# q loaded in 2 KB pieces and sorted at eviction, with an earlier start of the products, smaller preparation steps and half-row stores, in a fused attention and expert-merge kernel

## Chip, cores, metric

One core of one Trainium2 chip. The metric is the device time of one execution, in microseconds. The six runs of the kernel before lie within 0.3% (1258.14 to 1261.69 us). Each chip job also ran the kernel before on the same chip, several times. A ratio is the mean time of one kernel's fast runs over that of the kernel before in the same rounds, with a 95% interval. So it is not quite the ratio of the medians that are quoted beside it. Line numbers such as L347 differ between kernels, because the text above them differs. L93 is in all of them a helper that issues every tensor-tensor operation, so those are told apart by their tiles. In the views PE is TensorE, PEld its weight loads, DVE VectorE, ACT ScalarE, POOL GpSimd and SP the engine that issues most loads. In this kernel TensorE writes its results to PSUM, to tiles that the code calls banks; an **eviction** is the copy or addition that moves a result from PSUM to SBUF, the on-chip memory, and frees the bank.

## The reference

```python
# lightning attention: B=4, H=8, S=768, D=64, fp32, chunk by chunk
intra = (q_b k_b^T * decay mask) v_b
inter = (q_b * lam^(pos+1)) kv_state
kv_state = lam^block * kv_state + (k_b * lam^(block-1-pos))^T v_b
x = (intra + inter) as (B*S, H*D) = (3072, 512)
# then 4 experts, F = 1024, weighted by normalised domain probabilities
out = sum_e p_e * (relu(x @ w1[e]) @ w2[e])
```

All inputs are fp32 in HBM. q, k and v lie as (batch, head, token, 64), so one row of a head is 256 B, and consecutive tokens of one head are contiguous.

## The kernel before

The kernel takes 128 tokens at a time (a chunk, all 8 heads) and writes the attention's result, transposed, to `xT`. Eight chunks make a group of 1024 tokens. Both expert products use Strassen-like schemes of seven products (M1 to M7). The sums that they need of x, w1 and w2 are made by GpSimd and VectorE as "chores" that a function `pump` issues between matmuls. The results go to HBM and are fetched again just ahead of use. The first group's attention runs alone (the **opening**, about the first 110 us). The other two groups' attention is spread in small steps between the matmuls of the expert products (the **middle**).

The parts that the change touches, with cuts marked by `...`:

```python
def load(n):                                   # 128 tokens of q, k, v
    b, c = divmod(n, NCH)
    for name, src in (("q", q), ("k", k), ("v", v)):
        x = small(f"{name}n")[:].rearrange("p (h d) -> p h d", d=D)
        nc.sync.dma_start(out=x, in_=src[b, :, c*C:(c+1)*C, :].rearrange("h p d -> p h d"))
...
def pump():                                    # the stores of the last chore, then one chore
    for f in stores: f()
    stores.clear()
    if chores: chores.pop(0)()
...
def turn(n, tags):                             # transpose q and k of a chunk
    for x, y in ((qp, qn), (kp, kn)):
        for hp in range(NHP):
            nc.tensor.transpose(out=x[:, hp*C:(hp+1)*C], in_=y[:, 2*hp:2*hp+2]..., identity=ident[:])
    nc.scalar.copy(out=qT[:], in_=qp[:])       # one copy of 128x512
    nc.scalar.copy(out=kT[:], in_=kp[:])
    if n % NCH:
        tt(nc.vector, qs[:], qT[:], q_decay..., ALU.mult)
...
def scores(n, tags):   # TensorE: k^T q per head; VectorE: st = scores * mask
def values(n, tags):   # TensorE: result and new kv; ScalarE: copy to xT; VectorE: kv update
...
for x, part in enumerate(order):               # one product of a unit: 8 places
    ...
    if x in (1, 4, 6):
        pump()
```

Of the kernel before, what the change touches and what calls it, by code (L numbers as in the profile page):

```python
# [20 lines left out]
def kernel(  # L21
# [30 lines left out]
    nc = tc.nc  # L52
# [45 lines left out]
    def load(n):  # L98
        b, c = divmod(n, NCH)
        tiles = []  # L100
        for name, src in (("q", q), ("k", k), ("v", v)):
            x = small(f"{name}n")[:].rearrange("p (h d) -> p h d", d=D)
            nc.sync.dma_start(out=x, in_=src[b, :, c * C:(c + 1) * C, :].rearrange("h p d -> p h d"))  # L103
            tiles.append(x)
        nat[n] = tiles
# [3 lines left out]
    lam_hp = consts.tile([P, NHP], FP32, name="lam_hp")  # L109
    for hd in range(2):  # L110
        nc.scalar.dma_start(
            out=lam_hp[half[hd], :], in_=lam.rearrange("(hp hd) -> hd hp", hd=2)[hd].partition_broadcast(D),
        )
# [56 lines left out]
    def prepare_w1(e):  # L170
# [13 lines left out]
        def ready(m):  # L184
# [5 lines left out]
            lambda: (total("S1", "A21", "A22", ALU.add), ready("M5")),  # L190
            lambda: (total("S3", "A11", "A21", ALU.subtract), ready("M7")),
            lambda: (total("S2", "S1", "A11", ALU.subtract), block("A12", 0, 1), ready("M6")),
            lambda: ready("M2"),
            lambda: (total("S4", "A12", "S2", ALU.subtract), ready("M3")),
# [41 lines left out]
    def prepare_x(g):  # L236

        st = {}

        def total(name, a, b, op):  # L240
            t = stage.tile([P, 2, W], FP32, name="xo", tag="st")
            tt(nc.gpsimd, t[:], a, b, op)
            st[name] = t[:]

        def ready(m, blk):
            inner_x(nc.gpsimd, g, m, blk)

        return [lambda: ready("M1", b11), lambda: ready("M2", b21)], [
            lambda: (total("T1", b12, b11, ALU.subtract), ready("M5", st["T1"])),
            lambda: (total("T2", b22, st["T1"], ALU.subtract), ready("M6", st["T2"])),  # L250
            lambda: (total("T3", b22, b12, ALU.subtract), ready("M7", st["T3"])),
            lambda: ready("M3", b22),
            lambda: (total("T4", b21, st["T2"], ALU.subtract), ready("M4", st["T4"])),
        ]
# [29 lines left out]
    for n in range(4):  # L284
        load(n)
    for name in ("A21", "A22", "A11"):
        raw_w1(0, name)
    probs = consts.tile([P, NTOK // P, E], FP32, name="probs")
    nc.scalar.dma_start(out=probs[:], in_=moe_domain_probs.rearrange("(t p) e -> p t e", p=P))
# [16 lines left out]
    nc.vector.tensor_copy(out=q_decay[:, :, 0], in_=lam_hp[:])  # L306
# [11 lines left out]

    gate = consts.tile([P, NTOK // P, E], FP32, name="gate")
# [16 lines left out]
    def turn(n, tags):  # L336
        qn, kn, _ = nat[n]
        qp = bank(tags[0], "qp")
        kp = bank(tags[1], "kp")
        for x, y in ((qp, qn), (kp, kn)):  # L340
            for hp in range(NHP):
                nc.tensor.transpose(  # L342
                    out=x[:, hp * C:(hp + 1) * C], in_=y[:, 2 * hp:2 * hp + 2].rearrange("p h d -> p (h d)"),
                    identity=ident[:],
                )
        qT, kT, qs = small("qT"), small("kT"), None
        nc.scalar.copy(out=qT[:], in_=qp[:])  # L347
# [26 lines left out]
    def values(n, tags):  # L374
        _, kn, vn = nat.pop(n)
# [198 lines left out]
    def second_product(g, e, m, banks):  # L574

        def part(sj, s):
# [29 lines left out]
            if e == E - 1 and m in ("M5", "M3"):  # L606
                nc.gpsimd.dma_start(out=out[n * P:(n + 1) * P, :], in_=acc.pop(n)[0][:])  # L607
# [16 lines left out]
    def direct_product(e, m, blocks, tags):  # L624
# [6 lines left out]
        def quarter(at):  # L631
# [9 lines left out]
            new[at] = small("m" + at) if m in ("M1", "M2", "M5") else blocks[old][at]  # L641
            if old is None:
# [10 lines left out]
    between, blocks = [], {}  # L653
    for i in range(CPG + 2):
        if i == 3:
            sum_w1(0, "S1", "A21", "A22", ALU.add)
            sum_w1(0, "S3", "A11", "A21", ALU.subtract)
        if i == 4:
# [3 lines left out]
        if i > 4:  # L662
            pump()
        if i == 6:
            between = direct_product(0, "M1", blocks, ("g1", "g3"))
        for f, lag in ((scores, 1), (turn, 0), (values, 2)):
# [3 lines left out]
            if i == 7 and lag == 0:  # L670
                between += direct_product(0, "M2", blocks, ("g1", "g3"))
            if between:
                between.pop(0)()
        if i + 4 < CPG:
            load(i + 4)
        if i == 0:
            raw_w1(0, "A12")
        if i == 6:
            gates()

    def sum_x(name, a, b):
        t = stream.tile([P, 7, 256], FP32, name="xt", tag="xw"[len(x_now) % 2])
        x_now[name] = t[:, 0:4].rearrange("p (c a) t -> p c (a t)", c=2)
        tt(nc.vector, x_now[name], x_now[a], x_now[b], ALU.subtract)

    sum_x("T1", "B12", "B11")
    sum_x("T2", "B22", "T1")
    sum_x("T3", "B22", "B12")
    sum_x("T4", "B21", "T2")
    for f in between:  # L690
        f()
    chores.extend(lambda n=n: raw_w1(1, n) for n in ("A11", "A12", "A21", "A22"))
    chores.append(lambda: sum_w1(1, "S1", "A21", "A22", ALU.add))
    for m in SEQ0[2:]:
# [9 lines left out]
        lambda: sum_w1(1, "S3", "A11", "A21", ALU.subtract), own[1], w2_steps[0],  # L704
        lambda: sum_w1(1, "S4", "A12", "S2", ALU.subtract), own[2], w2_steps[1],
        own[3], w2_steps[2], w2_steps[3], own[4], w2_steps[4], w1_steps[0], own[5], *w1_steps[1:3], own[6], *w1_steps[3:],
# [6 lines left out]
    for at, (g, e) in enumerate(units):  # L713
# [9 lines left out]
        for i in range(7):  # L723
# [11 lines left out]
            for x, part in enumerate(order):  # L735
# [10 lines left out]
                if x in (1, 4, 6):  # L746
                    pump()
    assert not (background or chores or stores or acc)
# [28 lines left out]
```

## Time and profile before

| | before |
|---|---|
| time, median of the first 3 runs | 1260.18 us |
| span of the profiled run | 1257.4 us |
| TensorE busy | 1226.8 us (98%) |
| TensorE waits | 25.7 us, of which 16.1 in the opening |
| tail after the last matmul | 4.9 us |

TensorE bounds the kernel, so what counts is its idle time. A line of waits reads "engine, tile and line, what it waited for: us in total, times, longest us". A line of stretches reads "window, length, busy us of PE, PEld, DVE, ACT and POOL with their instructions, granted clock, DMA share, GB/s". A line of a tile or group gives count and min/median/max of the duration in ns.

```profile
L347 ACT COPY qT<-qp x24: 566/585/592, 5.8 to 674.6; 128x512 f32<-128x512 f32 x24
```

```profile
DVE qs L93 <- ACT qT L347: 13.6, 16, 3.2
```

The first line has a granted clock of 0.83: TensorE idles here for 3.3 us ahead of the first matmul that needs a sum of x. The line of L347 is the single copy that evicts q, 585 ns.

### The profile page before, as it was taken

What the parts mean: (1) busy time and instruction counts of PE and PEld (TensorE: products, weight loads), DVE (VectorE), ACT (ScalarE), POOL (GpSimd) and SP (SyncE); (2) the same over time, 40 slices, a digit from 0 to 9 for tenths busy, and PEclk for the clock granted to TensorE, in tenths of its full rate; (3) what the DMA queues carried; (4) which work ended last, traced back from release to release, by engine and by line L of the source; (5) the groups of instructions that cost most, each with busy time, mean ns of one, the idle gap of its engine ahead of it and who ended that gap; (6) DMA issues with size and microseconds to landing.
All of it is one profiled execution on the core that took longest, in us unless ns stands there. A gap on an engine that the chain in (4) does not pass through costs nothing.

```text
span 1257.4 us, 16224 instructions
## 1 busy us (share of the span) xinstructions
PE 1226.8 (98%) x6376; PEld 1071.3 (85%) x6376; DVE 762.4 (61%) x1267; ACT 217.1 (17%) x361; POOL 301.1 (24%) x294
## 2 busy tenths in 40 slices
PE   6989999999999999999999999999999999999998
PEld 5878888888888888888888888888888888888887
DVE  4656478477467745756764674674764755755742
ACT  2213102111202211220221021120120120220100
POOL 3620236586356683112000700000010000000001
PEclk9999999999999999999999999999999999999999
DMA  9741477999999799667544764454565445454412
GB/s 187 209 151 47 166 251 270 374 317 382 307 341 348 225 328 362 214 222 237 176 176 151 265 232 177 175 202 154 217 224 199 178 174 203 154 217 156 167 59 93
DMA packets 173052, 273.10 MB, mean 217 GB/s; under 512 B 87600, under 2 KB 120496, under 8 KB 172976
## 3 DMA queue, kind: packets, MB, share of 16 engines
q1 hardware_dynamic: 143808, 212.37, 50.6%
q10 hardware_dynamic: 27248, 53.41, 11.3%
q0 software_dynamic: 1920, 6.29, 1.3%
q8 instruction: 50, 0.82, 0.3%
q14 instruction: 26, 0.21, 0.1%
HBM read 212.39 MB, written 59.64 MB: 216 GB/s over the span
## 4 chain that ended last, share of the span: by engine, by line
PE 47%; issue 42%; DMA 5%; POOL 2%; SPq 2%; DVE 1%; ACT 0%; ACTq 0%; POOLq 0%; DVEq 0%
PE q L589 18%; PE pg L537 14%; PE pM L637 7%; PE op L389 2%; PE sp L365 2%; PE kvp L398 2%; SPq L103 1%; PE op L383 1%; DMA xs_in<-x_ops 1%; DMA x_ops<-xo 1%; DMA w2t<-in_moe_w_dram 1%; POOL ops L93 1%; POOL out_dram L607 1%; PE qp L342 1%; DMA kn<-in_k_dram 1%
## 5 line engine op out<-in xcount | busy, mean ns | idle before, releaser
L537 PE MATMUL pg<-xs_in,ws_in 128*128 128x256 f32 x1960 | 470.9, 380 | 6.6 <-DVE m L93 3.4
L537 PEld LDWEIGHTS pg<-xs_in,ws_in 128*128 128x128 f32 x1960 | 369.2, 190 | 60.3 <-DVE m L93 5.6
L589 PE MATMUL q<-w2t,hS 128*128 128x256 f32 x1536 | 361.0, 379 | 0.0
L93 DVE TENSOR_TENSOR m<-pg,m 128x512 f32<-128x512 f32 x410 | 280.1, 688 | 92.9 <-PE pg L537 79.2
L589 PEld LDWEIGHTS q<-w2t,hS 128*128 128x128 f32 x1536 | 291.1, 190 | 39.9
L605 DVE SCALAR_TENSOR_TENSOR acc<-q,gate,acc 128x256 f32<-128x256 f32 x288 | 138.9, 482 | 234.6 <-PE q L589 234.2
L589 PE MATMUL q<-w2t,m 128*128 128x256 f32 x1152 | 270.7, 379 | 0.0
L589 PEld LDWEIGHTS q<-w2t,m 128*128 128x128 f32 x1152 | 218.5, 190 | 29.7
L607 POOL DMA_DIRECT2D out_dram<-acc x24 | 13.2, 550 | 548.6 <-DVE acc L605 548.6
L549 ACT ACTIVATE m<-m 128x512 f32<-128x512 f32 x120 | 75.4, 630 | 361.9 <-DVE m L93 349.7
L93 DVE TENSOR_TENSOR hS<-m,m 128x512 f32<-128x512 f32 x96 | 68.8, 719 | 20.9 <-ACT m L549 20.9
L545 ACT COPY m<-pg 128x512 f32<-128x512 f32 x80 | 46.5, 585 | 174.9 <-PE pg L537 157.1
L93 DVE TENSOR_TENSOR m<-m,m 128x512 f32<-128x512 f32 x96 | 73.8, 773 | 0.0
L93 POOL TENSOR_TENSOR kn<-kn,s_decay 128x256 f32<-128x256 f32 x40 | 30.1, 773 | 114.1 <-PE kp L342 110.9
L491 ACT ACTIVATE m<-m 128x512 f32<-128x512 f32 x48 | 29.9, 629 | 152.3 <-DVE m L93 147.7
L637 PE MATMUL pM<-xt,w1o 128*128 128x256 f32 x192 | 45.6, 391 | 4.8 <-DVE xt L93 3.3
L637 PEld LDWEIGHTS pM<-xt,w1o 128*128 128x128 f32 x192 | 37.2, 196 | 10.7 <-DVE xt L93 3.5
L602 DVE TENSOR_SCALAR acc<-q,gate 128x256 f32<-128x256 f32 x48 | 23.1, 482 | 37.2 <-PE q L589 37.1
L93 DVE TENSOR_TENSOR m<-pM,m 128x512 f32<-128x512 f32 x40 | 27.4, 687 | 24.9 <-PE pM L637 24.8
L93 DVE TENSOR_TENSOR st<-sp,s_decay 128x512 f32<-128x512 f32 x48 | 30.8, 684 | 11.4 <-PE sp L365 11.2
L93 DVE TENSOR_TENSOR hS<-hS,m 128x512 f32<-128x512 f32 x48 | 35.3, 736 | 0.5
L93 POOL TENSOR_TENSOR w2o<-w2b 128x1024 f32<-128x1024 f32 x8 | 18.9, 2364 | 69.4 <-DMA w2b<-in_moe_w_dram 49.9
(65 smaller groups left out, 777.4 us busy)
## 6 DMA issues: line engine op xcount, KB each, us to landing
xs_in<-x_ops SPq DMA_DIRECT2D x70, 896.0 KB, 4.6
ws_in<-w_ops SPq DMA_DIRECT2D x70, 896.0 KB, 6.6
w2t<-w_sums SPq DMA_DIRECT2D x96, 256.0 KB, 6.4
w2t<-in_moe_w_dram SPq DMA_DIRECT2D x72, 256.0 KB, 6.6
w_ops<-ops ACTq DMA_DIRECT2D x28, 512.0 KB, 6.8
x_ops<-ops ACTq DMA_DIRECT2D x21, 512.0 KB, 5.0
w2b<-in_moe_w_dram SPq DMA_DIRECT2D x32, 256.0 KB, 5.6
w_sums<-w2o ACTq DMA_DIRECT2D x16, 512.0 KB, 6.7
```

The lines of the kernel that those rows point to most:

```text
L93: eng.tensor_tensor(out=o, in0=a, in1=b, op=op)
L365: nc.tensor.matmul(out=sp[hd][:, hp * C:(hp + 1) * C], lhsT=hc(kT)[half[hd], hp], rhs=hc(qT)[half[hd], hp], start=True, stop=True,)
L389: nc.tensor.matmul(out=op[half[hd], hp * C:(hp + 1) * C], lhsT=vn[:, 2 * hp + hd], rhs=hc(st[hd])[:, hp], start=(first and hp == 0), stop= ...
L398: nc.tensor.matmul(out=kpv[:, hp], lhsT=kn[:, 2 * hp:2 * hp + 2].rearrange("p h d -> p (h d)"), rhs=vn[:, 2 * hp:2 * hp + 2].rearrange("p ...
L491: nc.scalar.activation(out=o[:], in_=o[:], func=AF.Relu)
L537: nc.tensor.matmul(out=p[:, j * 256:(j + 1) * 256], lhsT=ws[:, W1_AT[i], j * P:(j + 1) * P], rhs=xs[:, X_AT[i]], start=(fresh and j == 0), ...
L545: nc.scalar.copy(out=new[at][:], in_=p[:])
L549: nc.scalar.activation(out=new[at][:], in_=new[at][:], func=AF.Relu)
L589: nc.tensor.matmul(out=p[:, s * DH:(s + 1) * DH], lhsT=h[A_OF[m]][:, c * 256 + s * P:c * 256 + (s + 1) * P], rhs=fed2[g, e, m][uu][:, c], ...
L605: nc.vector.scalar_tensor_tensor(out=o, in0=x, scalar=w, in1=o, op0=ALU.mult, op1=ALU.add)
L607: nc.gpsimd.dma_start(out=out[n * P:(n + 1) * P, :], in_=acc.pop(n)[0][:])
L637: nc.tensor.matmul(out=p[:, s * 256:(s + 1) * 256], lhsT=a[c][:, f:f + P], rhs=b[:, c, j * 256:(j + 1) * 256], start=(s == 0 and c == 0), ...
```

## The change

The intent: start the opening earlier, fill its gaps with matmuls that need no sum of x, keep GpSimd from falling behind, and shorten the tail. The diff, cut to its core:

```diff
-    def load(n):
+    def load(n, names="qkv"):
...
+            if name == "q":      # partition = (head, block of 8 tokens): 128 pieces of 2 KB
+                nc.sync.dma_start(out=x[:], in_=src.rearrange("h (tb ti) d -> h tb (ti d)", ti=TI))
-    lam_hp = consts.tile([P, NHP], FP32, name="lam_hp")       # and its two loads
...
-    for n in range(4):
-        load(n)
-    for name in ("A21", "A22", "A11"):
-        raw_w1(0, name)
-    nc.scalar.dma_start(out=probs[:], ...)                    # now after iteration 5
+    for n, names in ((0, "qk"), (1, "qk"), (0, "v"), (2, "qk"), (1, "v")):
+        load(n, names)
+    raw_w1(0, "A11")
+    load(3, "qk")
...
     def turn(n, tags):
-        nc.scalar.copy(out=qT[:], in_=qp[:])
+        to = qT[:].rearrange("p (hp tb u r) -> p r u hp tb", hp=NHP, tb=TB, r=2)
+        of = qp[:].rearrange("p (u hp hd tb) -> p hd u hp tb", u=TI // 2, hp=NHP, hd=2)
+        for hd in range(2):
+            for r in range(2):
+                nc.scalar.copy(out=to[half[hd], r], in_=of[half[r], hd])   # 4 copies of 64x256
...
-            lambda: (total("S1", "A21", "A22", ALU.add), ready("M5")),
+            lambda: total("S1", "A21", "A22", ALU.add), lambda: ready("M5"),      # and the like
...
-            if e == E - 1 and m in ("M5", "M3"):
-                nc.gpsimd.dma_start(out=out[n * P:(n + 1) * P, :], in_=acc.pop(n)[0][:])
+            if e == E - 1 and m in ("M2", "M4", "M5", "M3"):
+                queue = nc.sync if (g, m) == (NG - 1, "M3") else nc.gpsimd
+                queue.dma_start(out=out[n * P:(n + 1) * P, j * DH:(j + 1) * DH], in_=o)
...
+    between = {4: (m1[0], m1[2]), 5: (m2[0], m2[2]), 6: (m1[1],), 7: (m1[3],), 8: (m2[1],), 9: (..., m2[3])}
...
-                if x in (1, 4, 6):
+                if x % 2 == 0:
                     pump()
```

More of the change, by code (lines that the diff above doesn't have):

```diff
@@ L96 @@
     nat = {}
-    def load(n):
+    TI = 8
+    TB = C // TI
+    def load(n, names="qkv"):
         b, c = divmod(n, NCH)
-        tiles = []
-        for name, src in (("q", q), ("k", k), ("v", v)):
-            x = small(f"{name}n")[:].rearrange("p (h d) -> p h d", d=D)
-            nc.sync.dma_start(out=x, in_=src[b, :, c * C:(c + 1) * C, :].rearrange("h p d -> p h d"))
-            tiles.append(x)
-        nat[n] = tiles
+        for name in names:
+            x = small(f"{name}n")
+            src = {"q": q, "k": k, "v": v}[name][b, :, c * C:(c + 1) * C, :]
+            if name == "q":
+                nc.sync.dma_start(out=x[:], in_=src.rearrange("h (tb ti) d -> h tb (ti d)", ti=TI))
+                nat[n, name] = x
+            else:
+                nat[n, name] = x[:].rearrange("p (h d) -> p h d", d=D)
+                nc.sync.dma_start(out=nat[n, name], in_=src.rearrange("h p d -> p h d"))
     lam_bc = consts.tile([P, H], FP32, name="lam_bc")
     nc.scalar.dma_start(out=lam_bc[:], in_=lam.partition_broadcast(P))
-    lam_hp = consts.tile([P, NHP], FP32, name="lam_hp")
-    for hd in range(2):
-        nc.scalar.dma_start(
-            out=lam_hp[half[hd], :], in_=lam.rearrange("(hp hd) -> hd hp", hd=2)[hd].partition_broadcast(D),
-        )
     w1_ops = dram.tile([E, 7, P, 7, 256], FP32, name="w1_ops")
@@ L189, in prepare_w1 @@
             lambda: ready("M1"),
-            lambda: (total("S1", "A21", "A22", ALU.add), ready("M5")),
-            lambda: (total("S3", "A11", "A21", ALU.subtract), ready("M7")),
-            lambda: (total("S2", "S1", "A11", ALU.subtract), block("A12", 0, 1), ready("M6")),
+            lambda: total("S1", "A21", "A22", ALU.add), lambda: ready("M5"),
+            lambda: total("S3", "A11", "A21", ALU.subtract), lambda: ready("M7"),
+            lambda: (total("S2", "S1", "A11", ALU.subtract), block("A12", 0, 1)), lambda: ready("M6"),
             lambda: ready("M2"),
-            lambda: (total("S4", "A12", "S2", ALU.subtract), ready("M3")),
+            lambda: total("S4", "A12", "S2", ALU.subtract), lambda: ready("M3"),
             lambda: ready("M4"),
@@ L248, in prepare_x @@
         return [lambda: ready("M1", b11), lambda: ready("M2", b21)], [
-            lambda: (total("T1", b12, b11, ALU.subtract), ready("M5", st["T1"])),
-            lambda: (total("T2", b22, st["T1"], ALU.subtract), ready("M6", st["T2"])),
-            lambda: (total("T3", b22, b12, ALU.subtract), ready("M7", st["T3"])),
+            lambda: total("T1", b12, b11, ALU.subtract), lambda: ready("M5", st["T1"]),
+            lambda: total("T2", b22, st["T1"], ALU.subtract), lambda: ready("M6", st["T2"]),
+            lambda: total("T3", b22, b12, ALU.subtract), lambda: ready("M7", st["T3"]),
             lambda: ready("M3", b22),
-            lambda: (total("T4", b21, st["T2"], ALU.subtract), ready("M4", st["T4"])),
+            lambda: total("T4", b21, st["T2"], ALU.subtract), lambda: ready("M4", st["T4"]),
         ]
@@ L282, in sum_w1 @@
         w1_now[e][name] = to
-    for n in range(4):
-        load(n)
-    for name in ("A21", "A22", "A11"):
-        raw_w1(0, name)
-    probs = consts.tile([P, NTOK // P, E], FP32, name="probs")
-    nc.scalar.dma_start(out=probs[:], in_=moe_domain_probs.rearrange("(t p) e -> p t e", p=P))
+    for n, names in ((0, "qk"), (1, "qk"), (0, "v"), (2, "qk"), (1, "v")):
+        load(n, names)
+    raw_w1(0, "A11")
+    load(3, "qk")
+    load(2, "v")
+    raw_w1(0, "A12")
+    load(3, "v")
+    raw_w1(0, "A21")
+    raw_w1(0, "A22")
     s_decay = consts.tile([P, 2, NHP, C], FP32, name="s_decay")
@@ L305 @@
     q_decay = consts.tile([P, NHP, C], FP32, name="q_decay")
-    nc.vector.tensor_copy(out=q_decay[:, :, 0], in_=lam_hp[:])
+    for hd in range(2):
+        nc.vector.tensor_copy(
+            out=q_decay[half[hd], :, 0], in_=lam_bc[half[hd], :].rearrange("p (hp hd) -> p hd hp", hd=2)[:, hd],
+        )
     m = 1
@@ L317 @@
     nc.vector.memset(kv[:], 0.0)
+    probs = consts.tile([P, NTOK // P, E], FP32, name="probs")
     gate = consts.tile([P, NTOK // P, E], FP32, name="gate")
@@ L336, in turn @@
     def turn(n, tags):
-        qn, kn, _ = nat[n]
+        qn, kn = nat.pop((n, "q")), nat[n, "k"]
         qp = bank(tags[0], "qp")
         kp = bank(tags[1], "kp")
-        for x, y in ((qp, qn), (kp, kn)):
-            for hp in range(NHP):
-                nc.tensor.transpose(
-                    out=x[:, hp * C:(hp + 1) * C], in_=y[:, 2 * hp:2 * hp + 2].rearrange("p h d -> p (h d)"),
-                    identity=ident[:],
-                )
-        qT, kT, qs = small("qT"), small("kT"), None
-        nc.scalar.copy(out=qT[:], in_=qp[:])
+        for hp in range(NHP):
+            nc.tensor.transpose(out=qp[:, hp * C:(hp + 1) * C], in_=qn[:, hp * C:(hp + 1) * C], identity=ident[:])
+        for hp in range(NHP):
+            nc.tensor.transpose(
+                out=kp[:, hp * C:(hp + 1) * C], in_=kn[:, 2 * hp:2 * hp + 2].rearrange("p h d -> p (h d)"),
+                identity=ident[:],
+            )
+        qT, kT, qs = small("qT"), small("kT"), None
+        to = qT[:].rearrange("p (hp tb u r) -> p r u hp tb", hp=NHP, tb=TB, r=2)
+        of = qp[:].rearrange("p (u hp hd tb) -> p hd u hp tb", u=TI // 2, hp=NHP, hd=2)
+        for hd in range(2):
+            for r in range(2):
+                nc.scalar.copy(out=to[half[hd], r], in_=of[half[r], hd])
         nc.scalar.copy(out=kT[:], in_=kp[:])
@@ L374, in values @@
     def values(n, tags):
-        _, kn, vn = nat.pop(n)
+        kn, vn = nat.pop((n, "k")), nat.pop((n, "v"))
         qs = turned.pop(n)[2]
@@ L641, in quarter @@
             new[at] = small("m" + at) if m in ("M1", "M2", "M5") else blocks[old][at]
+            if m == "M1":
+                blocks[m] = new
             if old is None:
@@ L652, with x_sums @@
     pairs = (("s0", "s1"), ("q01", "q02"), ("q11", "q12"))
-    between, blocks = [], {}
+    def x_sums():
+        for name, a, b in (("T1", "B12", "B11"), ("T2", "B22", "T1"), ("T3", "B22", "B12"), ("T4", "B21", "T2")):
+            t = stream.tile([P, 7, 256], FP32, name="xt", tag="xw"[len(x_now) % 2])
+            x_now[name] = t[:, 0:4].rearrange("p (c a) t -> p c (a t)", c=2)
+            tt(nc.vector, x_now[name], x_now[a], x_now[b], ALU.subtract)
+    blocks = {}
+    m1, m2 = (direct_product(0, m, blocks, ("g1", "g3")) for m in ("M1", "M2"))
+    between = {
+        4: (m1[0], m1[2]), 5: (m2[0], m2[2]), 6: (m1[1],), 7: (m1[3],), 8: (m2[1],), 9: (lambda: None, lambda: None, m2[3]),
+    }
     for i in range(CPG + 2):
-        if i == 3:
+        if i == 4:
             sum_w1(0, "S1", "A21", "A22", ALU.add)
             sum_w1(0, "S3", "A11", "A21", ALU.subtract)
-        if i == 4:
+        if i == 5:
             sum_w1(0, "S2", "S1", "A11", ALU.subtract)
@@ L661 @@
             chores.extend(prepare_w2(0))
-        if i > 4:
+        if i > 5:
             pump()
-        if i == 6:
-            between = direct_product(0, "M1", blocks, ("g1", "g3"))
+        more = list(between.get(i, ()))
         for f, lag in ((scores, 1), (turn, 0), (values, 2)):
@@ L669 @@
                 f(n, pairs[n % 3])
-            if i == 7 and lag == 0:
-                between += direct_product(0, "M2", blocks, ("g1", "g3"))
-            if between:
-                between.pop(0)()
+            if i == 9 and lag == 2:
+                x_sums()
+            if more:
+                more.pop(0)()
         if i + 4 < CPG:
             load(i + 4)
-        if i == 0:
-            raw_w1(0, "A12")
-        if i == 6:
+        if i == 5:
+            nc.scalar.dma_start(out=probs[:], in_=moe_domain_probs.rearrange("(t p) e -> p t e", p=P))
+        if i == 9:
             gates()
-    def sum_x(name, a, b):
-        t = stream.tile([P, 7, 256], FP32, name="xt", tag="xw"[len(x_now) % 2])
-        x_now[name] = t[:, 0:4].rearrange("p (c a) t -> p c (a t)", c=2)
-        tt(nc.vector, x_now[name], x_now[a], x_now[b], ALU.subtract)
-    sum_x("T1", "B12", "B11")
-    sum_x("T2", "B22", "T1")
-    sum_x("T3", "B22", "B12")
-    sum_x("T4", "B21", "T2")
-    for f in between:
-        f()
+    m1[4]()
+    m2[4]()
     chores.extend(lambda n=n: raw_w1(1, n) for n in ("A11", "A12", "A21", "A22"))
@@ L703 @@
         lambda: sum_w1(1, "S2", "S1", "A11", ALU.subtract), own[0],
-        lambda: sum_w1(1, "S3", "A11", "A21", ALU.subtract), own[1], w2_steps[0],
-        lambda: sum_w1(1, "S4", "A12", "S2", ALU.subtract), own[2], w2_steps[1],
-        own[3], w2_steps[2], w2_steps[3], own[4], w2_steps[4], w1_steps[0], own[5], *w1_steps[1:3], own[6], *w1_steps[3:],
+        lambda: sum_w1(1, "S3", "A11", "A21", ALU.subtract), own[1], own[2],
+        lambda: sum_w1(1, "S4", "A12", "S2", ALU.subtract), own[3], own[4], *w2_steps[:2], own[5], *w2_steps[2:], own[6],
+        *w1_steps,
     ))
@@ L745 @@
                     steps.pop(0)()
-                if x in (1, 4, 6):
+                if x % 2 == 0:
                     pump()
-    assert not (background or chores or stores or acc)
+    assert not (background or chores or stores)
 _INS = ['q', 'k', 'v', 'lam', 'moe_domain_probs', 'moe_w1', 'moe_w2']
```

## The prediction

> **What bounds the kernel now.** I read the page first (busy shares, then slices), then the waits of the tensor engine, the table of stretches, and the timeline around each wait. From the page of the kernel before:
>
> ```profile
> PE 1226.8 (98%) x6376; PEld 1071.3 (85%) x6376; DVE 762.4 (61%) x1267; ACT 217.1 (17%) x361; POOL 301.1 (24%) x294
> ...
> PE   6989999999999999999999999999999999999998
> ...
> PEclk9999999999999999999999999999999999999999
> ```
>
> TensorE is busy 98% of 1257.4 us at full granted clock; the other engines are at 61% and below. The diff neither adds nor removes a matmul or a transpose. So it can only take from the 1257.4 - 1226.8 = 30.6 us in which PE is idle[...]. Where those 30.6 us are is told by the waits of PE, all eight of them:
>
> ```profile
> PE qp L342 <- DMA qn<-in_q_dram: 8.4, 3, 4.7
> PE pg L537 <- DVE m L93: 3.4, 4, 1.8
> PE pM L637 <- DVE xt L93: 3.3, 1, 3.3
> PE pg L537 <- ACT m L545: 3.1, 2, 2.2
> PE sp L365 <- ACT kT L348: 3.0, 3, 1.7
> PE kp L342 <- DMA kn<-in_k_dram: 2.1, 2, 1.6
> PE pM L637 <- DVE m L93: 1.5, 1, 1.5
> PE kp L342 <- PE qp L342: 0.9, 1, 0.9
> ```
>
> They sum to 25.7 us; the remaining 4.9 us are the tail after the last matmul (it ends at 1252.5). By the same view cut to windows, the opening (to 75 us) holds 8.4 + 2.1 + 0.9 + 3.3 + 1.4 (two of the three kT waits) = 16.1 us; 9.6 us lie between 155 and 550 us; none after. Why the opening waits for q and k is seen in the table of stretches and in the transfers of the first 16 us:
>
> ```profile
> 0.00:10.00 10.00, 3.03 (x16) 2.26 (x18) 3.13 (x10) 2.45 (x3) 1.90 (x8) 1.00 0.46 83
> 10.00:20.00 10.00, 6.88 (x43) 5.56 (x42) 5.09 (x13) 1.41 (x3) 1.20 (x2) 1.00 1.35 196
> ```
>
> ```profile
> q1 hardware_dynamic: 7345, 1.85, 65.6%
> q10 hardware_dynamic: 3776, 0.06, 14.6%
> ...
> probs<-in_moe_domain_probs_dram ACTq DMA_DIRECT2D x1, 48.0 KB, 10.1
> lam_hp<-in_lam_dram ACTq DMA_DIRECT2D x2, 1.0 KB, 6.7
> ```
>
> The last two columns of a stretch are the DMA share and GB/s: 83 GB/s in the first 10 us. The second queue sends 3776 packets for 0.06 MB: the gate probabilities in 16-byte pieces and lambda in 4-byte pieces, between the first loads of q, k and v. In the timeline the second q lands only at 13.65 us.
>
> [...]q, k and v go in 256 B pieces (1024 per 256 KB load) and 10 to 20 us gave 196 GB/s, while 220 to 240 us, with larger pieces, gave 366. [...]four transposes take 1.09 to 1.12 us up to 18.6 us and 0.60 to 0.66 later, sixteen score matmuls 2.08 against 1.16. [...]the trace has 585 for the q eviction. [...]a 128x512 add that takes 0.68 us took 2.81 us at 371.03 beside a 2.35 us GpSimd sum.
>
> **The change part by part.**
>
> 1. *Opening loads.* q goes as 128 pieces of 2 KB instead of 1024 of 256 B; the two lambda loads go, and the probabilities move behind iteration 5. The order becomes q0 k0 q1 k1 v0 q2 k2 v1, with the w1 blocks in between. Before, turn 0 ran at 4.69 (q) and 7.38 (k), turn 1 at 13.65, values 0 at 20.28. After, by estimate: first q at 3.5 (the smallest load in the trace, lam_bc, takes 3.3 us to land), k0 at 5.0, then a k or v every 1.2 to 1.3 us (256 KB at 196 to 217 GB/s) and a q every 0.7 (at 366). So: k transposes 5.0 to 6.1, kT copy (0.58) to 6.7, scores to 8.8, turn 1 8.8 to 11.0 with no wait for data (k1 is due near 7), scores 1 from 12.1 to 14.2, turn 2 to 16, values 0 at 16. Gain at this point 20.3 - 16.1 = **4.2 us**.[...]
>
> 2. *Iterations 4 and 5.* Before, they still waited 1.29, 0.45 and 0.87 us for q and k. After, some 5.6 MB lie ahead of k4; at 250 GB/s that is 22 us, so k4 lands near 25 while its turn, behind a quarter of M1, comes near 26. Gain **2.6 us**, with thin margin.
>
> 3. *q eviction.* One copy of 128x512 (585 ns, 24 of them) becomes four of 64x256, because the new layout mixes two tokens per transpose.[...] Off the path, except where scores follow their turn closely: iteration 1, where only PE's k transposes lie between. That wait, 0.7 before, becomes 1.1 (already in part 1). From iteration 2 on, values (2.2 to 3.3 us) lie between.
>
> 4. *Early quarters of M1, M2 and the x sums.* The same quarters run, in iterations 4 to 9 instead of 6 to 8. What matters is one: M2's last quarter now comes after the last values, where PE waited 3.3 us for the first x sum (VectorE must finish four kv updates, then 1.72 us of sum). A quarter is 1.73 us (8 matmuls). The wait falls to 1.6: gain **1.7 us**. The gates' 2.9 us of VectorE move behind the sums, so they don't add to it.
>
> 5. *Smaller preparation steps, four pumps per eight places instead of three.* Before, one chore was a GpSimd sum (2.36 us) plus four half sums (0.73 each, 2.9), so 5.3 us, while a pump came each 14/3 = 4.6 us (a product is about 13.9 us); GpSimd fell behind, ScalarE's in-order queue sat in front of a store, and evictions behind it came late. The timeline shows that before 219.66 (0.9 us), 444.20 (2.2) and 484.27 (1.8, the q copy 3.2 us late). Now the chores average 2.6 us against a pump every 3.5. Of the 9.6 us I expect a good half to go: **5 us**. This is a choice, not a count: [...]the q copies sit in that queue too.
>
> 6. *Stores by halves.* 24 POOL stores of 256 KB become 48 of 128 KB, the last four from the sync queue. Extra issue time of 24 x 0.55 = 13 us on an engine that idles at the end. Only the tail counts: the last issue took 0.54 us on POOL and landing 2.3 us; SP issues take 0.3 to 0.4. Gain **0.5 us**.
>
> Sum: 4.2 + 2.6 + 1.7 + 5 + 0.5 = 14.0 us, so 1260.2 - 14.0 = **1246.2 us**.
>
> **The rivals.** (a) *The opening turns into a wait on ScalarE.* The loads come early, but four copies a turn, k's copy, the x eviction and the quarters' copies are [...]all in one in-order queue. For: the kT waits that exist.[...] If it costs 1 us in each of four iterations: 1250. (b) *The middle waits stay or move.* For: [...]all preparation work remains. Against: the ratio of chore to pump falls from above 1 to below. If nothing is gained there: 1251; if all goes: 1242. (c) *The transfers were hidden anyway.* Against: the four DMA lines of the waits are real PE idle; but if the first arrival is bound by latency and not by packets, part 1 is 2 us smaller: 1248.[...]
>
> **Range and chances.** Idle that cannot go: first data 3.5, k0 and first scores 1.2, x sum 1.6, a tail of 4, in all 10 us; so at most some 20 of 30.6 us[...]. Parts 1, 2 and 4 alone give 1251.7. I take 1240 to 1252. Over 2% faster means below 1235, beyond the idle that can go: 0.02. Slower by over 2% needs 25 us of new waits with nothing to cause them: 0.01.
>
> **What would show it.** Part 1: over 150 GB/s in the first 10 us and values 0 near 16 us. Part 2: no q or k wait after turn 1. Part 3: four q copies near 0.4 us each. Part 4: an x-sum wait near 1.6 us and the first M5 matmul near 65.3 us (73.82 before). Part 5: PE waits after 150 us of 4 to 5 us in place of 9.6. Part 6: tail near 4.4 us. Wrong would make it: new PE waits on ACT qT or kT, on GpSimd's late w1 sums, or on the own x sums that wait for a staging buffer.

What no trace or run of this case shows is cut from it, and the cuts are marked: general statements about the hardware (the traced figures beside them stay; the 585 for the q eviction is in ns), how the length of a q copy was worked out with ScalarE's time that followed from it, parts of rivals (a) and (b) and of part 5, and all of rival (d) with its 2 us of the range. No term of the sum is cut: 4.2 + 2.6 + 1.7 + 5 + 0.5 = 14.0 us, which gives 1246.2 us. The 0.4 us forecast for a q copy, and with it 0.4 us of longer wait before the second scores in part 1, are my bare estimate.

## More of the kernel before

The prediction shows the main lines of this kernel. More become important later. They come from the table of stretches and from VectorE's waits (the line from the view of the tile qT stands above):

```profile
70.00:80.00 10.00, 6.72 (x26) 5.46 (x26) 9.19 (x11) 1.28 (x3) 2.68 (x3) 0.83 0.25 78
```

## The result

The changed kernel took **1260.67 us** (median of 6 runs, 1260.17 to 1261.9) against 1260.16 us of the kernel before (6 runs, 1258.14 to 1261.69). The ratio is 1.0006, with an interval from 0.9993 to 1.0019. Nothing was gained. The time lies above the predicted 1246.2 us and outside its range of 1240 to 1252; that the change stays within 2% came true.

The same views of the changed kernel. From the page, and TensorE's waits (all of them):

```profile
PE 1226.9 (97%) x6376; PEld 1071.1 (85%) x6376; DVE 758.7 (60%) x1268; ACT 263.2 (21%) x433; POOL 306.5 (24%) x314
```

```profile
PE pg L552 <- DVE m L93: 8.2, 8, 2.2
PE qp L350 <- DMA qn<-in_q_dram: 6.6, 1, 6.6
PE sp L380 <- ACT kT L363: 5.6, 3, 2.3
PE pg L552 <- ACT m L560: 5.1, 5, 1.8
PE pM L653 <- DVE m L93: 1.2, 1, 1.2
PE op L398 <- DVE kv L420: 1.1, 1, 1.1
PE pM L653 <- DVE xt L93: 0.9, 1, 0.9
```

The waits for k and the later q are gone, as predicted. But the single wait for the first q is longer (6.6 us; 4.7 before), the scores wait 5.6 us for kT (3.0 before), and the two lines of `pg`, the expert products of the middle, went from 6.5 us to 13.3. From the table of stretches:

```profile
0.00:10.00 10.00, 1.94 (x8) 1.57 (x8) 4.99 (x18) 3.53 (x5) 1.90 (x8) 1.00 0.61 137
10.00:20.00 10.00, 6.79 (x44) 5.94 (x45) 2.68 (x5) 3.84 (x7) 1.20 (x2) 1.00 0.87 210
```

The DMA moved more (137 GB/s in the first 10 us; 83 before), yet TensorE did no more in 20 us (1.94 + 6.79 us busy; 3.03 + 6.88 before). After the first q, loads stopped being what it waits for. What it waits for instead is in the views of qT and of VectorE's waits:

```profile
L362 ACT COPY qT<-qp x96: 597/620/632, 7.7 to 679.6; 64x256 f32<-64x256 f32 x96
```

```profile
DVE qs L93 <- ACT qT L362: 52.9, 20, 5.5
```

One q copy takes 0.62 us, not the forecast 0.4 (my estimate, with no trace behind it), and there are four, so a q takes 2.5 us instead of 0.585. ScalarE's busy time grew by 46 us (217.1 to 263.2). VectorE's wait for qT grew from 13.6 to 52.9 us. How that reaches TensorE is seen in the timeline of one turn in the middle (start us, busy us, engine, line, operation, tiles, and in brackets the idle time before it and its releaser):

```profile
605.43 2.51 ACT L362 COPY qT<-qp 64x256 f32<-64x256 f32 x4 [0.86 <-PE qp L350]
...
607.97 0.69 DVE L93 TENSOR_TENSOR qs<-qT,q_decay 128x512 f32<-128x512 f32 x1 [2.54 <-ACT qT L362]
608.58 0.68 DVE L93 TENSOR_TENSOR m<-pg,m 128x512 f32<-128x512 f32 x1
...
609.32 1.99 PE L552 MATMUL pg<-xs_in,ws_in 128*128 128x256 f32 x8 [0.95 <-DVE m L93]
```

TensorE finished the q transposes at about 605.3. ScalarE copies until 607.94. VectorE has the `qs` multiply next in its order and idles 2.54 us for qT. The addition behind it (`m<-pg`), which would empty a PSUM bank, starts only at 608.58. TensorE needs that bank for the next `pg` matmuls and stands still for 0.95 us. With one copy, the kernel before has no wait of TensorE after 546 us. The longest of these waits, 2.21 us at 372.20, shows more: there the late `qs` ran beside a GpSimd sum of 2.36 us and took 1.94 us instead of 0.69.

For the comparison of all runs I cut the span at two marks of the timeline: the start of the first matmul of the second product (end of the opening), and the start of the last VectorE operation (end of the middle). The rest is the tail.

| kernel (profiled run) | opening | middle | tail | span |
|---|---|---|---|---|
| before | 111.9 | 1140.6 | 4.9 | 1257.4 |
| after | 108.9 | 1146.7 | 3.4 | 1259.0 |

So the opening gave 2.9 us and the tail 1.5, and the middle took 6.1 back.

### The profile page after: what moved, and what is told of

It reads as the page before. It is cut to its first block, busy times and chain, and to the rows that moved or that the text cites. A ratio compares the mean times of both kernels' runs of the same rounds, so it can differ in the third digit from the quotient of the medians.

```text
span 1259.0 us, 16340 instructions
## 1 busy us (share of the span) xinstructions
PE 1226.9 (97%) x6376; PEld 1071.1 (85%) x6376; DVE 758.7 (60%) x1268; ACT 263.2 (21%) x433; POOL 306.5 (24%) x314
## 4 chain that ended last, share of the span: by engine, by line
PE 87%; DMA 3%; ACT 3%; POOL 2%; DVE 2%; issue 2%; ACTq 0%; SPq 0%; POOLq 0%; DVEq 0%
PE q L604 42%; PE pg L552 32%; PE pM L653 6%; ACT qT L362 2%; PE sp L380 2%; PE op L404 2%; PE kvp L413 1%; PE op L398 1%; DMA xs_in<-x_ops 1%; DMA w_ops<-ops 1%; POOL w1o L93 1%; POOL ops L93 1%; PE qp L350 1%; DMA w_ops<-w1o 1%; DVE kv L93 1%
## 5 line engine op out<-in xcount | busy, mean ns | idle before, releaser
L552 PE MATMUL pg<-xs_in,ws_in 128*128 128x256 f32 x1960 | 471.4, 380 | 13.3 <-DVE m L93 8.2
L623 POOL DMA_DIRECT2D out_dram<-acc x44 | 24.1, 548 | 551.7 <-DVE acc L620 551.7
L362 ACT COPY qT<-qp 64x256 f32<-64x256 f32 x96 | 59.5, 619 | 88.6 <-PE qp L350 47.9
L93 POOL TENSOR_TENSOR kn<-kn,s_decay 128x256 f32<-128x256 f32 x40 | 24.9, 644 | 119.3 <-PE kp L352 106.9
L93 DVE TENSOR_TENSOR qs<-qT,q_decay 128x512 f32<-128x512 f32 x20 | 18.6, 930 | 52.9 <-ACT qT L362 52.9
L408 ACT COPY xT<-op 128x512 f32<-128x512 f32 x24 | 14.0, 585 | 116.0 <-PE op L404 62.1
L93 DVE TENSOR_TENSOR st<-sp,s_decay 128x512 f32<-128x512 f32 x48 | 30.9, 685 | 11.8 <-PE sp L380 11.7
```

The source lines that it names most:

```text
L93: eng.tensor_tensor(out=o, in0=a, in1=b, op=op)
L362: nc.scalar.copy(out=to[half[hd], r], in_=of[half[r], hd])
L552: nc.tensor.matmul(out=p[:, j * 256:(j + 1) * 256], lhsT=ws[:, W1_AT[i], j * P:(j + 1) * P], rhs=xs[:, X_AT[i]], start=(fresh and j == 0), ...
L623: queue.dma_start(out=out[n * P:(n + 1) * P, j * DH:(j + 1) * DH], in_=o)
```

## The experiments

**Theory A:** the four strided copies of q are the loss. They lengthen the chain to the first scores in the opening and, through VectorE's in-order wait for qT, hold PSUM banks in the middle. Without them the change would be worth what was predicted. **Rival B:** the smaller steps and the fourth pump made the new waits of the middle. **Rival C:** the 2 KB load itself is slow, whatever evicts it.

### q as before, all else changed

```diff
-            if name == "q":
-                nc.sync.dma_start(out=x[:], in_=src.rearrange("h (tb ti) d -> h tb (ti d)", ti=TI))
+            nat[n, name] = x[:].rearrange("p (h d) -> p h d", d=D)
+            nc.sync.dma_start(out=nat[n, name], in_=src.rearrange("h p d -> p h d"))
...
-        for hd in range(2): for r in range(2): nc.scalar.copy(...)
+        nc.scalar.copy(out=qT[:], in_=qp[:])
```

> The changed kernel with q loaded in 256 B pieces and evicted by one ScalarE copy again; all else of the change stays. Theory A (the four copies of 0.62 us hold VectorE's qs multiply and with it the evictions that TensorE waits for, and hold the scores in the opening): PE waits after 150 us fall from about 14.5 us to below 6, the two kT waits of the opening from 2.3 to under 1 us each, time near 1250 us. Rival B (the smaller steps and the more frequent pumps made the new middle waits): the middle stays at 12 us or more, time 1258 or above. First q should land near 4.7 us again.

Measured: 1240.25 us, ratio 0.9841 (0.9824 to 0.9859). Two later jobs ran the same kernel again, for comparison on their chips:

> The variant with q as before once more, so that the next three are compared on the same chip: ratio near 0.984, about 1240 us.

Measured: 1240.59 us, 0.9847 (0.9832 to 0.9861).

> The variant with q as before, for comparison on the same chip: ratio near 0.9845.

Measured: 1242.67 us, 0.9861 (0.9842 to 0.988).

TensorE's waits of the first of these runs:

```profile
PE qp L347 <- DMA qn<-in_q_dram: 4.8, 1, 4.8
PE pg L542 <- ACT m L550: 3.1, 1, 3.1
PE pg L542 <- DVE m L93: 3.0, 4, 1.4
PE sp L370 <- ACT kT L353: 1.3, 2, 0.7
PE op L388 <- DVE kv L410: 1.1, 1, 1.1
PE pM L643 <- DVE xt L93: 0.9, 1, 0.9
```

The two `pg` waits fell from 13.3 to 6.1 us and the scores' wait from 5.6 to 1.3. The time is 10 us below the expected 1250. In these three runs q costs the changed kernel 1.0006 - 0.985 = 0.0156 of 1260 us, about **20 us**, and the rest of the change is worth about 19. Theory A stands, for the q part as a whole; load and copies are told apart further down. Rival B falls: with its steps and pumps in place the middle is 1133 to 1137 us, below the 1140.6 of before.

### The q part alone, on the kernel before

The diff is the reverse: the kernel before, with the new q load and the four copies.

> The kernel before with only q's loading and eviction changed (its order of loads and its lambda and probabilities loads stay). Theory A: slower than before by 5 to 12 us (1265 to 1272), with some 10 to 14 new waits of about 0.95 us before pg matmuls behind a qs multiply that waits for qT. Rival B: within 3 us of before.

Measured: 1278.01 us, ratio 1.0144 (1.0129 to 1.0159), so 18 us slower, beyond the expected 5 to 12. Opening 116.5 us (111.9 before), middle 1155.4 (1140.6). The loss shows without any other part of the change. VectorE's `pg` waits were 8 (8.8 us), not the expected 10 to 14. The record shows what I had not expected: one wait of 5.59 us for kT at 317.94 us (1.67 at the same scores before). There the q transposes ended at 306.7 us, but the q copies began only at 314.81, behind stores at 310.06 and 313.90 in ScalarE's queue; the profile names a GpSimd sum as what ended ScalarE's wait. So this run's loss may hold some that the copies make only together with the old preparation steps; it is not told apart.

### The multiply behind the masks

The four copies stay; only the `qs` multiply moves on VectorE.

```diff
     def turn(n, tags):
-        if n % NCH: qs = q * decay              # VectorE waits here for the four copies
     def scores(n, tags):
             tt(nc.vector, st[hd][:], sp[hd][:], s_decay..., ALU.mult)
+        if n % NCH: qs = q * decay              # by now qT is long there
```

> The changed kernel with the qs multiply issued after the scores' masks instead of at the turn, so VectorE never waits for the q copies ahead of an eviction; the four copies stay. Theory A in its narrow form (PE waits through VectorE's in-order wait for qT): the waits of pg on DVE after 250 us (8.2 us in all) fall below 3, time about 1255. Rival: ScalarE's own queue (evictions behind the copies, 5.1 us of pg on ACT) is what counts, and the time stays within 2 us of 1260.7.

Measured: 1253.78 us, ratio 0.9957 (0.9942 to 0.9972). The `pg` waits on VectorE fell from 8.2 to 1.9 us; the middle is 1140.6 us instead of 1146.7, the opening 107.6. So the in-order wait of VectorE is worth about 6 us. The `pg` waits on ScalarE stayed (5.2 us; 5.1 before this edit). In the timeline, three of the four (2.5 us in all) are evictions that stand right behind the q and kT copies in ScalarE's own queue. The fourth and longest, 2.73 us at 219.65, is not: its eviction stands behind a store of weight sums that was issued only at 218.65. That wait is there with q as before too (2.2 to 3.1 us near 213), so the copies don't make it.

### Why a copy takes 0.62 us

The same four copies, walked in another order: tokens innermost, so SBUF is written with a step of 2 elements (8 B) instead of 8 (32 B), and PSUM is read with a step of 128.

```diff
-        to = ... "p (hp tb u r) -> p r u hp tb"
-        of = ... "p (u hp hd tb) -> p hd u hp tb"
+        to = ... "p (hp tb u r) -> p r hp tb u"
+        of = ... "p (u hp hd tb) -> p hd hp tb u"
```

> The changed kernel with the four q copies walking in another order: PSUM read with a step of 128 elements, SBUF written with a step of 2 elements, instead of read in rows of 16 and written with a step of 8. If the 0.62 us of a copy[...] comes from the wide step of the write, it falls towards 0.40 us, and the time falls by about half of what q costs, to 1250; if the number of instructions or the partitions is the cause, it stays 0.62 us and 1260.

Measured: 1252.41 us, ratio 0.9947 (0.9932 to 0.9962). The view of qT:

```profile
L362 ACT COPY qT<-qp x96: 362/387/405, 7.7 to 669.6; 64x256 f32<-64x256 f32 x96
```

0.39 us a copy instead of 0.62, as many copies on as many partitions, and 7.4 us of time ((1.0006 - 0.9947) x 1260). Next, four copies without any reordering, on the variant with q as before:

```diff
-        nc.scalar.copy(out=qT[:], in_=qp[:])
+        for hd in range(2):
+            for s in range(2):
+                sl = slice(s * 2 * C, (s + 1) * 2 * C)
+                nc.scalar.copy(out=qT[half[hd], sl], in_=qp[half[hd], sl])
```

> The variant with q as before (ratio 0.984), its q eviction cut into four copies of 64x256 without reordering (right result). It prices the number of copies apart from their pattern:[...] time 1243 to 1249, between the two; if a copy takes 0.62 here too, the pattern is not to blame and the time is that of the changed kernel less the opening's difference, about 1257.

Measured: 1243.53 us, ratio 0.9875 (0.986 to 0.989).

```profile
L355 ACT COPY qT<-qp x96: 347/367/377, 5.7 to 660.9; 64x256 f32<-64x256 f32 x96
```

0.367 us. So the number of copies costs some 3 us at most here (0.9875 against 0.985, from other jobs; the interval overlaps that of the third run with q as before). The rest of a copy's length goes with the pattern of the write: 0.62 us with 32 B, with PSUM read in rows of 16 or, in the next experiment, with a step of 8; 0.39 us with 8 B; 0.37 us in a row. The runs change the step together with the order in which the write walks its rows, so the step isn't isolated, and why a step of 32 B is slower is not shown. Reading PSUM with a step of 128 and writing with a step of 2, both together, cost ScalarE only 0.02 us.

### Why the 2 KB load is slow

First with 16 rows in the outermost dimension of the load, instead of 8 heads:

```diff
-                src.rearrange("h (tb ti) d -> h tb (ti d)", ti=TI)      # 8 x 16 pieces
+                src.rearrange("h (tb ti) d -> tb h (ti d)", ti=TI)      # 16 x 8 pieces
-        of = qp[:].rearrange("p (u hp hd tb) -> p hd u hp tb", ...)
+        of = qp[:].rearrange("p (u tb hp hd) -> p hd u hp tb", ...)
```

> The changed kernel with q's partitions ordered token block first, so that the outermost dimension of its load has 16 rows instead of 8 heads; the eviction reads PSUM with a stride of 8 elements instead of along the row. [...]the first q lands 1 to 2 us earlier than 6.6 us; rival: it lands at the same time, and the late landing comes from the loads issued right behind it. The time of one copy tells whether reading PSUM in a row matters (0.62 us now). Total within 2 us of the changed kernel.

Measured: 1259.82 us, ratio 1.0002 (0.9984 to 1.002). The first q came at 5.6 us instead of 6.6, a copy still took 0.62 us, and the time didn't move: the scores' wait for kT is the same 5.6 us, so the copies still bound the opening. The load can only be priced with the copies out of the way. So, with a **wrong result**, the changed kernel with one plain copy (the tokens of q stay unsorted):

```diff
-        for hd in range(2): for r in range(2): nc.scalar.copy(out=to[half[hd], r], in_=of[half[r], hd])
+        nc.scalar.copy(out=qT[:], in_=qp[:])        # wrong order of tokens
```

> WRONG RESULT ON PURPOSE: the changed kernel with q loaded in 2 KB pieces but evicted unsorted by one copy of 128x512, to price the load alone. If 2 KB pieces help, it is faster than the variant with q as before (0.984 of the time before) by some us; theory now: the load gains nothing that the path needs and its first arrival is later (6.5 against 4.8 us), so 1240 to 1244, ratio 0.984 to 0.987.

Measured: 1246.7 us (1242.48 to 1249.4), ratio 0.9897 (0.9874 to 0.992), opening 105.9 us: slower than q as before, by more than expected. TensorE waited for q three times (9.0 us in all), once for 2.16 us at 28.7 us. And the same with 16 rows outermost, wrong result again:

> WRONG RESULT ON PURPOSE: q in 2 KB pieces with 16 rows outermost, evicted unsorted by one copy. If the 8 rows outermost made the load slow, this is 3 us or more faster than the same with 8 rows (ratio 0.9897) and near q as before (0.9845); if the pieces or their place in the queue are the cause, it stays near 0.9897.

Measured: 1241.05 us, ratio 0.9853 (0.9834 to 0.9873), opening 101.5 us. That equals q as before (0.9861 on the same chip); the two one-copy runs come from different jobs. So rival C is half right: **in its 8-row form the load costs about 5 us, in its 16-row form nothing, and in neither does it gain anything** over the 256 B pieces. The traces show a difference between the two forms. The pages of the changed kernel and of the 16-row run, whose loads and stores are otherwise the same:

```profile
DMA packets 151582, 273.12 MB, mean 217 GB/s; under 512 B 62672, under 2 KB 96080, under 8 KB 151504
```

```profile
DMA packets 151774, 273.12 MB, mean 217 GB/s; under 512 B 62864, under 2 KB 96272, under 8 KB 151696
```

The 16-row form has 192 more packets under 512 B, 8 for each of the 24 q loads. No view shows what they are, but the packet and semaphore records in the trace files do: they are 4 B each, and the first q load lands in 8 parts with 8 rows (4.7 to 5.7 us after its issue, besides one early update at 1.2 us), and in 16 parts with 16 rows (3.3 to 4.7 us). Whether the number of parts makes the 5 us is not shown. The first q alone doesn't carry the difference in time: it came at 6.4 us in this run.

Both faults mended in a kernel with the right result (16 rows outermost and a write step of 2):

> The changed kernel with both faults of the q part mended: 16 rows outermost in the load, and the copies written with a step of 2. Expected: first q at 5.6 us, copies of 0.39 us, about 1250 us (0.992), still slower than q as before, because four copies take 1.55 us where one takes 0.59. Rival: if it reaches 1241 or less, the 2 KB pieces are worth having and only their details were wrong.

Measured: 1248.79 us, ratio 0.9912 (0.9899 to 0.9926). It is 11.8 us better than the changed kernel ((1.0006 - 0.9912) x 1260) and still about 6 us behind q as before on the same chip (0.9861). The 16 rows give 4.4 us here as well ((0.9947 - 0.9912) x 1260, from two jobs). Four copies remain four copies: 4 x 0.387 = 1.55 us ahead of the scores and of the multiply, against 0.585. But what four copies cost stays open: 7.4 us against the one copy of the run before ((0.9912 - 0.9853) x 1260, same chip), at most some 3 us in the plain copies above. Part of the 7.4 us is what the delay happens to meet: in this run's profile TensorE waits 2.20 us at 367.51 behind a `qs` multiply that took 2.87 us beside a GpSimd sum of 2.34 us.

### The small packets of the opening

On the variant with q as before, lambda's second form and the probabilities are loaded at the start again:

```diff
+    for hd in range(2):
+        nc.scalar.dma_start(out=lam_hp[half[hd], :], in_=lam....partition_broadcast(D))
...
+    nc.scalar.dma_start(out=probs[:], in_=moe_domain_probs.rearrange("(t p) e -> p t e", p=P))
```

> The variant with q as before, with lambda's second form and the probabilities loaded at the start again (3776 small packets in the first microseconds in all). If those small packets are what held q and k back before, values 0 starts 3 to 4 us later than the 15.7 us it has now, and the time is 3 to 5 us above 1240; rival (the new order of loads alone made the gain): within 1 us of 1240.

Measured: 1248.79 us, ratio 0.9917 (0.9902 to 0.9932), against 0.9847 of q as before on the same chip: **8.8 us** ((0.9917 - 0.9847) x 1260) for 50 KB, more than the expected 3 to 5. (The edit also makes q's decay from lambda's second form again; no wait of TensorE in this run names it.) The first 10 us, with these loads and without them:

```profile
0.00:10.00 10.00, 2.81 (x14) 2.04 (x16) 3.00 (x9) 2.46 (x3) 1.89 (x8) 1.00 0.45 82
```

```profile
0.00:10.00 10.00, 4.81 (x28) 4.11 (x29) 5.60 (x18) 2.45 (x3) 1.90 (x8) 1.00 0.81 181
```

82 GB/s against 181, and TensorE 2.81 us busy against 4.81. The opening is 109.2 us against 101.8. So the small packets, some 3600 of them, and not the order of the loads, are what held q and k back before: TensorE's waits for them are 9.8 us in this run, 10.5 in the kernel before, and 6.5 without the packets.

### The stores, the smaller steps, and the multiply once more

All on the variant with q as before. The whole-row stores from GpSimd put back:

> The variant with q as before, with whole-row stores from GpSimd again. Predicted worth of the halves was 0.5 us; the profiles showed a tail shorter by 1.5 us. Expected 1 to 2 us above 1240, and a tail from the last VectorE operation of 4.9 us instead of 3.3.

Measured: 1242.68 us, ratio 0.9863 (0.9848 to 0.9878) against 0.9847 on the same chip. The tail is 4.8 us against 3.3. The intervals overlap; the tail's 1.5 us agree with the 2.1 us of the medians.

The old preparation steps and three pumps put back, in two jobs:

> The variant with q as before (ratio 0.984), with the preparation steps and the pumping of the kernel before put back. If the smaller steps are worth what was predicted, it is 3 to 6 us slower than 1240, with about 8 us of PE waits after 150 us instead of 6; if they are worth nothing, it stays at 1240.

Measured: 1245.65 us, ratio 0.9895 (0.9878 to 0.9911).

> The variant with q as before and the old preparation steps, on the same chip as f0. If the small steps and the fourth pump are worth 3 to 6 us, its ratio is 0.987 to 0.9895 against 0.9845 of f0; if nothing, the same.

Measured: 1244.19 us, ratio 0.987 (0.9851 to 0.9888), against 0.9861 on the same chip. The first comparison (with 0.9841, from another job) says 7 us, the second, on one chip, 1.5 us with overlapping intervals. **The worth of the smaller steps stays unsettled**, between nothing and 7 us.

The multiply behind the masks, with one copy:

> The variant with q as before, with the qs multiply after the scores' masks. If VectorE's in-order wait for qT still costs with one copy (0.6 us a turn), it is 1 to 4 us faster than 1240; if one copy is short enough, the same within 1 us. It is the candidate for a version that beats both kernels.

Measured: 1242.96 us, ratio 0.9866 (0.9852 to 0.9879) against 0.9847 and 0.9861 of q as before on the same chip. No gain is shown, and no loss: the intervals overlap. Where one copy takes 0.585 us, moving the multiply gives nothing that can be seen. The best version found remains **q as before with all the rest of the change: 1240 to 1243 us, 1.4 to 1.6% faster than both kernels.**

### All runs by parts

| kernel | ratio | opening | middle | tail |
|---|---|---|---|---|
| before | 1 | 111.9 | 1140.6 | 4.9 |
| after | 1.0006 | 108.9 | 1146.7 | 3.4 |
| q as before (three jobs) | 0.9841, 0.9847, 0.9861 | 101.4, 101.8, 102.3 | 1137.3, 1133.3, 1134.7 | 3.3, 3.3, 3.4 |
| before with the q part | 1.0144 | 116.5 | 1155.4 | 4.9 |
| multiply later | 0.9957 | 107.6 | 1140.6 | 3.7 |
| write step of 2 | 0.9947 | 105.2 | 1141.1 | 3.3 |
| 16 rows | 1.0002 | 107.9 | 1147.0 | 3.3 |
| 16 rows and write step of 2 | 0.9912 | 104.0 | 1140.8 | 3.3 |
| one copy, 8 rows (wrong result) | 0.9897 | 105.9 | 1136.1 | 3.3 |
| one copy, 16 rows (wrong result) | 0.9853 | 101.5 | 1133.3 | 3.3 |
| q as before, small packets early | 0.9917 | 109.2 | 1133.4 | 3.2 |
| q as before, four plain copies | 0.9875 | 101.1 | 1136.8 | 3.3 |
| q as before, old steps (two jobs) | 0.9895, 0.987 | 102.0, 101.8 | 1137.6, 1139.5 | 3.7, 3.7 |
| q as before, whole-row stores | 0.9863 | 101.3 | 1136.1 | 4.8 |
| q as before, multiply later | 0.9866 | 100.6 | 1137.7 | 3.3 |

## Why the prediction was wrong

- **Part 3, the q eviction, is the step that failed.** It put a copy "near 0.4 us", an estimate of mine without a trace behind it, and the extra ScalarE time "off the path, except where scores follow their turn closely". A copy took 0.62 us; with another pattern of reads and writes it took 0.39. And the path runs through it in the middle too: by VectorE's in-order wait for qT (about 6 us, the multiply-later run) and by evictions behind the copies in ScalarE's own queue (2.5 us in that run's profile). The prediction's own sign of being wrong, new waits for kT, came in the opening. Predicted cost 0.4 us; measured about 20, load included. I had looked at the share of ScalarE (17%) and not at who waits in order behind its copies.
- **Part 1** was right in its mechanism: the small packets cost 8.8 us, and with q as before the first values matmul runs at 15.69, 13.78 and 14.15 us in the three profiles (16 predicted, 20.28 before). In the changed kernel it ran at 21.09 us. "First q at 3.5" failed twice: 4.5 to 4.8 us with 256 B pieces, 6.6 us in the new form. The reading that the 196 GB/s of 10 to 20 us came from the 256 B pieces fails as well: with q in 256 B pieces and the small packets gone, that stretch moved 240 to 254 GB/s. The load in 2 KB pieces was taken as a gain; it gained nothing with 16 rows and cost about 5 us with 8.
- **Part 2** held: in the changed kernel no q or k wait is left after the first. Its thin margin showed with q as before, which comes to these loads sooner: two of the three profiles wait 1.7 us for a q near 26 us.
- **Part 4** was too small. The wait for the x sum fell from 3.3 to 0.9 us (1.6 predicted), and the granted clock didn't drop after it (1.00 from 70 to 80 us, 0.83 before). The first M5 matmul, forecast near 65.3 us, came at 72.58, and at 65.0 to 65.9 with q as before. From the first x-sum matmul to the end of the opening lie 21 quarters in both kernels: 38.05 us before (73.82 to 111.87), 36.36 after (72.58 to 108.94). The 1.7 us between them are slow clock: 0.50 from 74.6 to 78.0 us before, 1.00 from 72 to 80 us after. Gain 2.4 + 1.7 = 4.1 us, not 1.7.
- **Part 5** predicted 5 us and 4 to 5 us of waits after 150 us. The changed kernel had 14.5 us; with q as before 6.1, 3.8 and 4.8. The middle gained 3 to 7 us over before, but how much of it the steps made stays open. The one long wait left, 2.2 to 3.1 us near 213, is of the kind that this part described: an eviction behind a store in ScalarE's queue.
- **Part 6** predicted 0.5 us of tail, measured 1.5.
- Of the rivals, (a), a wait on ScalarE, named the right engine, but only for the opening and at 4 us. The opening lost about 7 us to the q part, the load included (108.9 against 101.4 to 102.3), the middle 9 to 13. (c) came true for the first q alone: with the small packets gone it came at 4.5 to 4.8 us, against 4.69 before. (d) expected TensorE's slower first operations to end earlier. They ended later: in the changed kernel, which has 2.3 us gaps before the scores, four transposes at 19.20 us still took 1.11 us (0.66 at 25.25) and sixteen values matmuls at 21.09 us took 1.98; with q as before those sixteen took 1.09 us at 15.69 us already.

Without the q part, the sum of 14 us would have been exceeded (about 19).

## What to carry to other kernels

An engine at 17% busy can still be the bound of a chain (the q part alone, four copies of 0.62 us for one of 0.585 with its load, cost 18 us): before you lengthen an instruction, list which engines wait in order behind its result, and which banks they empty. When an eviction reorders, try the loop order (0.62 us a copy with a write step of 32 B here, 0.39 us with 8 B), and price it with a short run or a row of the trace of that same pattern. Loads of many tiny packets belong behind the first large loads; 50 KB of them cost 7.4 of the 10 us that the opening could gain here.

## What stays open: the granted clock

TensorE's granted clock fell after some of its waits and not after others. In the kernel before it was 0.83 in the stretch with the wait of 3.3 us (70 to 80 us), and in the changed kernel, with a wait of 0.9 us there, 1.00. And four profiled runs differ at the same place in the timeline of TensorE (start us, busy us, and in brackets the wait). They are q as before in its first, second and third job, and the four plain copies:

```profile
213.88 3.40 PE L542 MATMUL pg<-xs_in,ws_in 128*128 128x256 f32 x8 [3.12 <-ACT m L550]
```

```profile
213.37 1.99 PE L542 MATMUL pg<-xs_in,ws_in 128*128 128x256 f32 x8 [2.20 <-ACT m L550]
```

```profile
214.63 1.99 PE L542 MATMUL pg<-xs_in,ws_in 128*128 128x256 f32 x8 [3.00 <-ACT m L550]
```

```profile
208.96 3.48 PE L545 MATMUL pg<-xs_in,ws_in 128*128 128x256 f32 x8 [1.93 <-ACT m L553]
```

The same eight matmuls took 3.40 or 3.48 us after waits of 3.12 and 1.93 us, with a granted clock of 0.66 in those 5 us, and 1.99 us at a clock of 1.00 after waits of 2.20 and 3.00 us. So the length of the wait alone does not decide it, and what does stays open. The drop costs 1.4 to 1.5 us, and it comes and goes between executions of one kernel. The profiles of the whole-row stores, of the second run with old steps and of the later multiply with one copy have it too (3.42 to 3.78 us), so differences of 1 to 2 us between those variants are not safe.
